# Turns at a shared port kept by semaphores, and a planner's times changed, in an attention and mixture-of-experts kernel

## The chip, the core and the metric

The kernel runs on one core of a Trainium2 chip. The core has five engines that run beside each other, each working through its own queue of instructions in order: TensorE (PE in the profile; PEld is its loading of weights), VectorE (DVE), ScalarE (ACT), GpSimd (POOL) and SyncE (SP, which here issues transfers). They wait for each other by semaphores. The metric is the device time of one execution in microseconds (us); lower is better.

## What is computed

Attention with a bias made of running sums, for 8 batches of 8 heads, 576 positions and 64 numbers a head, and then a layer of 8 experts. Each expert takes 576 of the 4608 tokens, in the order of the sorted gate logits:

```
scores = q @ k^T / 8;  cum = cumsum(max(s, 0))
scores = where(causal, -1e9, scores + min(cum_k - cum_q, 0))
attn   = exp(scores - rowmax);  x = (attn / (sum + 1e-9)) @ v          # 4608 x 512
logits = x @ w_gate                                                    # 4608 x 8
walk over all (token, expert) by falling logit: take it if the token is free and the expert has < 576
out[token] = relu(x[token] @ w1[expert]) @ w2[expert]
```

## The kernel before

Each fp32 number is split into a high and a low fp16 part, and products are summed from three half-precision products. ScalarE makes the high part, VectorE the low part, as a subtraction that reads two operands from SBUF; these are "the splits": line 411 for queries and keys (into QK), line 444 for values (Vl).

Attention goes over 16 head groups, each of two half passes (32 in all). A half pass n has these steps:

- `load` and `vload`: SP fetches raw, rv; ACT and DVE split them; SP moves halves of QK between partitions (line 416); QK gets rows of running sums by DMA (line 397, from auxk, which `sums` makes on DVE at the start, lines 346 to 360).
- `spass`: PE writes score tiles into three buffers pss (lines 486, 502), DVE takes each tile's row maximum (line 471, which also frees the buffer). ACT (lines 518, 520), POOL (line 522, tile mp), PE (524) and ACT (526) turn the maxima, and a DMA puts them into QK.
- `sts`: PE writes the transposed scores into pst (lines 544 to 547, 587 to 589), ACT takes the exponential (line 555, P), POOL subtracts its high part to get the low part R (line 557, two SBUF operands).
- `pv`: PE multiplies with the values (lines 618 to 620) into po; `norm`: ACT and DVE scale (lines 641 to 649), giving xp.
- `turn`: PE turns xp (line 681), ACT copies it (687), PE makes the logits (692, 693), DVE adds them (lines 700 and 707).

Of the router, parts for batches 0 to 3 and 4 to 6 (`choose`, lines 874 to 886) run on DVE inside attention. Behind attention come a router for the first expert (326 to 351 us) and eight experts, whose tokens POOL gathers (line 1226) and scatters (line 1352), with the router of the next expert on DVE beside PE's matmuls (lines 1293, 1297, 1379).

What sets every order: class `Plan`. The program adds tasks with an engine, a duration, what they need, a priority and buffers from rings; `run` then takes at each step the task that can start first by a clock of its own, and `start` emits its instructions. The order of each engine's queue is the order of `start`. A task with `lock` (each GpSimd task that is no DMA, the splits, most of `choose`, the sums, and the set-up work that may go to either engine) starts no earlier than the end of the other engine's last locked task, kept in `port`; this is in the plan alone, and nothing on the chip keeps that turn. Line 707 is not locked. One `Plan` makes attention, a second one router and experts.

## Time and profile before

| | us |
|---|---|
| median of 3 runs (lowest 775.1, highest 777.54) | 777.54 |
| the profiled execution | 777.66 |
| its span, first to last instruction | 775.6 |
| busy in it: PE, DVE, ACT, POOL | 722.0 (93%), 598.2 (77%), 391.7 (50%), 335.3 (43%) |

So 2.1 us lie around the span. Stages of the span: set-up and start-up to about 60 us, steady attention to about 312, its end to 326, the first expert's router to 351, the experts to 766, and the last scatter to the end. "Busy" is the time in which an engine has an instruction; the matmuls' ends are modelled and lie some 0.16 us behind their turns. An instruction that is held up at the port stays "busy", so a port stall is read from an instruction that lasts longer than its like, and a semaphore wait is read as idle time.

### The profile page before, as it was taken

The page shows a single profiled execution, that of the slowest core. Times are in us where ns is not written, and L with a number is a line of the kernel's source. Part 1 is how long each engine was busy: PE and PEld are TensorE (multiplying, and loading weights), DVE is VectorE, ACT ScalarE, POOL GpSimd, SP SyncE. Part 2 cuts the span into 40 slices and gives each one's busy share as a digit, 9 for nine tenths or more (in the row PEclk, how much of TensorE's full clock was granted, in tenths as well). Part 3 has the DMA queues.
Part 4 walks back from the last instruction along what each step waited for, and adds up shares of the span by engine and source line. Part 5 has one row for each costly group of instructions (what it writes and reads, how often), then busy time and mean ns, then how long its engine had stood idle before and what let it go on. Part 6 is the DMA issues. An engine that isn't in the chain of part 4 may idle for free.

```text
span 775.6 us, 22590 instructions
## 1 busy us (share of the span) xinstructions
PE 722.0 (93%) x8726; PEld 454.9 (59%) x8726; DVE 598.2 (77%) x2014; ACT 391.7 (50%) x794; POOL 335.3 (43%) x428
## 2 busy tenths in 40 slices
PE   9789999999999999628998999999999999999995
PEld 3457788787888888416644544545445454454542
DVE  7889999999999996678895877969788795380110
ACT  3548888888888878405334323324244232461110
POOL 7648988788878988102032041140412224202011
PEclk9679999999999999858999999999999999999998
DMA  7897768686776511106157376394845639851000
GB/s 233 195 213 202 220 175 250 172 241 196 209 203 171 156 35 64 63 35 204 42 167 200 110 113 180 129 222 133 190 156 155 187 105 262 228 180 48 15 28 34
DMA packets 89733, 118.72 MB, mean 153 GB/s; under 512 B 39246, under 2 KB 55758, under 8 KB 89614
## 3 DMA queue, kind: packets, MB, share of 16 engines
q1 hardware_dynamic: 83116, 97.82, 46.1%
q0 software_dynamic: 5952, 19.00, 8.1%
q8 instruction: 68, 1.11, 0.6%
q10 hardware_dynamic: 558, 0.47, 0.2%
q14 instruction: 39, 0.32, 0.1%
HBM read 71.67 MB, written 19.10 MB: 117 GB/s over the span
## 4 chain that ended last, share of the span: by engine, by line
PE 54%; issue 19%; DVE 13%; DMA 5%; POOL 4%; ACT 2%; SPq 1%; POOLq 0%; ACTq 0%; DVEq 0%
PE psm L1293 13%; PE psm L1379 10%; DVE pss L471 5%; PE pst L545 4%; PE pst L544 4%; PE pss L502 3%; PE po L618 3%; PE po L620 2%; PE po L619 2%; POOL out_dram L1352 2%; POOL xg L1226 2%; PE psn L1297 2%; PE po L735 2%; PE pss L681 2%; DMA xg<-xs,ids 1%
## 5 line engine op out<-in xcount | busy, mean ns | idle before, releaser
L557 POOL TENSOR_TENSOR R<-P 128x512 f16<-128x512 f32 (+1 forms) x221 | 218.9, 1016 | 26.9 <-ACT P L555 25.2
L1293 PE MATMUL psm<-xT,w1p 128*128 128x512 f16 (+1 forms) x876 | 193.1, 353 | 1.3 <-DMA xT<-xg 0.8
L1379 PE MATMUL psm<-w2p,hT 128*128 128x512 f16 x768 | 174.4, 379 | 0.0
L555 ACT ACTIVATE P<-pst 128x512 f32<-128x512 f32 (+1 forms) x224 | 119.9, 555 | 25.0 <-PE pst L547 10.3
L1297 PE MATMUL psn<-xT,w1p 128*128 128x64 f16 x768 | 129.7, 193 | 0.0
L471 DVE CUSTOM_DVE_ANT_0 pss<-pss,mS 128x512 f32<-128x512 f32 (+3 forms) x256 | 122.7, 506 | 9.0 <-PE pss L502 8.0
L1293 PEld LDWEIGHTS <-w1p 128*128 128x128 f16 x876 | 79.2, 98 | 80.0 <-issue 1.9
L1352 POOL DMA_INDIRECT out_dram<-y,ids x40 | 39.8, 995 | 198.7 <-ACT y L1390 169.6
L1379 PEld LDWEIGHTS <-hT 128*128 128x128 f16 x768 | 69.0, 98 | 80.3 <-issue 4.4
L1226 POOL DMA_INDIRECT xg<-xs,ids x40 | 43.6, 1089 | 167.3 <-DVE ids L1184 67.3
L618 PE MATMUL po<-V,P 128*128 128x65 f16 x960 | 113.8, 196 | 1.4 <-DVE xp L649 1.0
L620 PE MATMUL po<-V,R 128*128 128x65 f16 x960 | 114.0, 194 | 0.4 <-POOL R L557 0.4
L619 PE MATMUL po<-Vl,P 128*128 128x64 f16 x960 | 113.6, 193 | 0.0
L544 PE MATMUL pst<-QK 70*128 70x64 f16 (+4 forms) x512 | 108.5, 252 | 1.2 <-ACT P L555 0.7
L545 PE MATMUL pst<-QK 128*128 128x64 f16 (+4 forms) x512 | 107.8, 251 | 0.0
L619 PEld LDWEIGHTS <-P 128*128 128x128 bf16 x960 | 90.0, 100 | 9.1 <-issue 2.8
L618 PEld LDWEIGHTS <-P 128*128 128x128 bf16 x960 | 90.4, 98 | 5.9 <-issue 1.8
L1313 ACT ACTIVATE hT<-psm 128x512 f16<-128x512 f32 x64 | 38.2, 597 | 108.1 <-PE psm L1293 88.3
L620 PEld LDWEIGHTS <-R 128*128 128x128 f16 x960 | 89.9, 97 | 0.6 <-POOL R L557 0.6
L1390 ACT ACTIVATE y<-psm 128x512 f32<-128x512 f32 x32 | 19.1, 597 | 122.0 <-PE psm L1379 108.1
L502 PE MATMUL pss<-QK 67*128 67x512 f16 (+3 forms) x256 | 72.6, 307 | 4.7 <-DVE mr L471 2.4
L1297 PEld LDWEIGHTS <-w1p 128*128 128x128 f16 x768 | 67.7, 98 | 1.3
(221 smaller groups left out, 1443.4 us busy)
## 6 DMA issues: line engine op xcount, KB each, us to landing
QK<-QK SPq DMA_DIRECT2D x120, 144.0 KB
wst<-in_w_dram SPq DMA_DIRECT2D x32, 512.0 KB
wst<-in_w_dram SPq DMA_DIRECT2D x64, 256.0 KB
raw<-in_q_dram SPq DMA_DIRECT2D x32, 288.0 KB
raw<-in_k_dram SPq DMA_DIRECT2D x32, 288.0 KB
rv<-in_v_dram SPq DMA_DIRECT2D x32, 288.0 KB
xs<-xp SPq DMA_DIRECT2D x32, 256.0 KB
xs<-xp SPq DMA_DIRECT2D x8, 128.0 KB
```

The source lines that it names most:

```text
L471: return pl.add("v", dur, lambda: nc.vector.tensor_tensor_reduce(ps(), ps(), mask, 1.0, init() if init else -3e38, OP.add, OP.max, mr.t[:, ...
L502: nc.tensor.matmul(ps.t[:, :n], F()[:, q0:q0 + 128], F()[:, k0:k0 + n], start=True, stop=True)
L544: nc.tensor.matmul(ps[:, c0:c0 + n], F()[:, ks:ks + 128], F()[:, q:q + n], start=True, stop=False)
L545: nc.tensor.matmul(ps[:, c0:c0 + n], G()[:, ks:ks + 128], G()[:, q:q + n], start=False, stop=not diag)
L555: e = pl.add("a", n / 1200 + 0.171, lambda: nc.scalar.activation(P.t[:, c0:c0 + n], ps.t[:, :n], AF.Exp, scale=1.0 / YS), [x] + fresh, pri ...
L557: sub = lambda eng: eng.tensor_tensor(R.t[:, c0:c0 + n], P.t[:, c0:c0 + n], strided_hi(P.t)[:, c0:c0 + n], op=OP.subtract)
L618: nc.tensor.matmul(o[:, i], H[:, c:c + 128], V.t[:, pr, sl], start=f, stop=False)
L619: nc.tensor.matmul(o[:, i, 0:64], H[:, c:c + 128], Vl.t[:, pr, sl], start=False, stop=False)
L620: nc.tensor.matmul(o[:, i], R.t[:, c:c + 128], V.t[:, pr, sl], start=False, stop=l)
L1293: nc.tensor.matmul(ps[:, tiles[0]:tiles[-1] + 1] if len(tiles) > 1 else ps[:, tiles[0]], lhs(f, c, a), xT.t[:, tiles[0]:tiles[-1] + 1, 4 * ...
L1297: nc.tensor.matmul(pt.t[:, 64 * f:64 * f + 64], lhs(f, c, a), xT.t[:, 4, 4 * b + c, 0:64], start=s, stop=e)
L1379: nc.tensor.matmul(py.t, hT.t[:, f, a, 128 * i:128 * i + 128], w2p.t[:, f, b], start=f == 0 and k == 0, stop=f == 7 and k == 2)
```

## The change

Three things change, all in `Plan`. First, the clock of the plan: a PE task lasts 1.6% longer, a step from PE to ACT and from ACT to POOL 0.05 us longer and from DVE to PE 0.01 us longer (`AFTER`), and the port comes free for the other engine 0.06 us later (`HAND`). Second, since these numbers set the order, queues of all five engines are re-ordered, in attention and in the experts (there POOL's order stays). Third, in attention's plan alone, each locked task's last instruction gets a dependency on the other engine's last locked instruction, which becomes a semaphore wait where no other wait implies it.

```diff
+    HAND = 0.06
+    tc = None
+    AFTER = {("t", "a"): 0.05, ("a", "p"): 0.05, ("v", "t"): 0.01}
...
+        self.held = dict(v=None, p=None)
...
         if e == "t":
-            return dur, dur + 0.19
+            return dur * 1.016, dur * 1.016 + 0.19
...
+        made = f()
         if x.lock and e in "vp":
-            self.port[e] = t + x.occ
+            self.port[e] = t + x.occ + self.HAND
+            if self.tc:
+                other = self.held["p" if e == "v" else "v"]
+                if other is not None:
+                    self.tc.add_manual_dep(made.ins, other.ins.name, mybir.DependencyInfo(
+                        mybir.DependencyClass.Sync, mybir.DependencyReason.SCHED_ONLY), reason="port")
+                self.held[e] = made
         self.count -= 1
-        f()
...
-            y.ready = max(y.ready, t + x.occ if order else x.end)
+            y.ready = max(y.ready, t + x.occ if order else x.end + self.AFTER.get((e, y.e), 0.0))
...
         self.pl = Plan()
+        self.pl.tc = tc
```

Lines of the kernel before are 11 higher in the changed one from about line 225 on (411 is 422, 444 is 455, 471 is 482, 557 is 568), and 3 to 10 higher ahead of that.

Place 1, DVE's queue in the start-up, where the sums (lines 357, 358), the first splits and the first row maximum stand. Before:

```order
L357 SCALAR_TENSOR_TENSOR xp0_117<-xp0_117 64x576 [waits DVE_49]
L258 MEMSET P1_102 128x64
L358 TENSOR_SCALAR xp0_117<-xp0_117 64x576 [waits DVE_49]
L258 MEMSET V1_96 128x18
L411 SCALAR_TENSOR_TENSOR QK0_91<-raw0_87,QK0_91 128x576 [waits DMAHW1_49,Activation_49]
L411 SCALAR_TENSOR_TENSOR QK0_91<-raw0_87,QK0_91 128x576 [waits DMAHW2_49,Activation_49]
L411 SCALAR_TENSOR_TENSOR QK0_91<-raw0_87,QK0_91 128x576 [waits DMAHW3_49,Activation_49]
L411 SCALAR_TENSOR_TENSOR QK0_91<-raw0_87,QK0_91 128x576 [waits DMAHW4_49,Activation_49]
L285 TENSOR_SCALAR QK1_92<-mZ_131,vec_138 6x2560
L471 ISA pss0_122,mr0_105<-pss0_122,mS_130 128x128 [waits PE_49,Pool_49]
```

The same place after:

```order
L368 SCALAR_TENSOR_TENSOR xp0_117<-xp0_117 64x576 [waits DVE_49]
L296 TENSOR_SCALAR QK1_92<-mZ_131,vec_138 6x2560
L369 TENSOR_SCALAR xp0_117<-xp0_117 64x576 [waits DVE_49]
L422 SCALAR_TENSOR_TENSOR QK0_91<-raw0_87,QK0_91 128x576 [waits DMAHW3_49,Activation_49]
L422 SCALAR_TENSOR_TENSOR QK0_91<-raw0_87,QK0_91 128x576 [waits DMAHW4_49,Activation_49]
L309 MEMSET QK1_92 128x8x64 [waits DVE_49]
L455 SCALAR_TENSOR_TENSOR Vl0_98<-rv0_89,V0_95 128x1152 [waits DMAHW1_49,DMAHW4_49,Activation_49,Pool_49]
L422 SCALAR_TENSOR_TENSOR QK1_92<-raw1_88,QK1_92 128x2x576 [waits DMAHW6_49,DMAHW5_49,Activation_49]
L482 ISA pss1_123,mr0_105<-pss1_123,mS_130 128x128 [waits PE_49]
```

The first value split and the first split of QK1 moved ahead of the first row maximum (before they stood behind 16 of them), and the set-up rows of QK1 and two splits moved in between the sums.

Place 2, SP's queue in the start-up, around the first moves inside QK1. Before:

```order
L440 DMA rv1_90<-in_v_dram 128x576 [waits DMAHW3_49]
L327 DMA wgf_137<-in_w_gate_dram 128x4x8 [waits DMAHW4_49]
L440 DMA rv0_89<-in_v_dram 128x576 [waits DMAHW6_49,DVE_49]
L416 DMA QK1_92<-QK1_92 64x2x576 [waits DMAHW7_49,Activation_49]
L416 DMA QK1_92<-QK1_92 64x2x576 [waits DMAHW0_49]
L416 DMA QK1_92<-QK1_92 64x2x576 [waits DMAHW1_49,Activation_49]
```

After:

```order
L427 DMA QK0_91<-QK0_91 64x576 [waits DMAHW3_49]
L427 DMA QK0_91<-QK0_91 64x576 [waits DMAHW4_49]
L427 DMA QK1_92<-QK1_92 64x2x576 [waits DMAHW6_49,Activation_49]
L427 DMA QK1_92<-QK1_92 64x2x576 [waits DMAHW0_49]
L427 DMA QK1_92<-QK1_92 64x2x576 [waits DMAHW2_49,Activation_49]
```

The moves of QK1 stood behind a second load into rv0, which waits for DVE's value split; now they stand right behind those of QK0, and that load comes 13 rows later.

Place 3, DVE's queue in the middle of attention, around the seventh value split. Before:

```order
L471 ISA pss0_122,mr1_106<-pss0_122,mS_130 128x256 [waits PE_49]
L471 ISA mr1_106 128x1
L471 ISA pss2_124,mr1_106<-pss2_124,mS_130 128x512 [waits PE_49]
L471 ISA mr1_106 128x1
L444 SCALAR_TENSOR_TENSOR Vl0_98<-rv0_89,V0_95 128x1152 [waits DMAHW7_49,DMAHW0_49]
L649 TENSOR_TENSOR xp1_118<-po1_129,xp1_118 128x5x64 [waits Activation_49]
```

After:

```order
L660 TENSOR_TENSOR xp1_118<-po1_129,xp1_118 128x5x64 [waits Activation_49]
L482 ISA pss2_124,mr2_107<-pss2_124,mS_130 128x256 [waits PE_49]
L482 ISA mr2_107 128x1
L455 SCALAR_TENSOR_TENSOR Vl0_98<-rv0_89,V0_95 128x1152 [waits DMAHW3_49,DMAHW2_49,Pool_49]
L422 SCALAR_TENSOR_TENSOR QK0_91<-raw0_87,QK0_91 128x2x576 [waits DMAHW5_49,DMAHW2_49]
L422 SCALAR_TENSOR_TENSOR QK0_91<-raw0_87,QK0_91 128x2x576 [waits DMAHW7_49,DMAHW0_49]
L482 ISA pss0_122,mr2_107<-pss0_122,mS_130 128x512 [waits PE_49]
```

The splits stood one by one among the row maxima (2 pairs in 44 places behind the start-up); now 7 triples, 6 pairs and 11 single ones, the first of a row waiting for POOL. Behind the start-up 22 of DVE's instructions in attention have a new wait for POOL.

The other side, POOL's queue near the same place, after:

```order
L568 TENSOR_TENSOR R1_104<-P1_102 128x512 [waits PE_49,Activation_49]
L533 TENSOR_TENSOR mp1_111<-ms1_109,mp1_111 128x10 [waits Activation_49,Pool_49]
L568 TENSOR_TENSOR R1_104<-P1_102 128x512 [waits Activation_49] x2
L568 TENSOR_TENSOR R1_104<-P1_102 128x512 [waits DVE_49,Activation_49]
L568 TENSOR_TENSOR R1_104<-P1_102 128x512 [waits Activation_49] x2
```

One R task in such a row now waits for DVE's last split; 21 of POOL's instructions have such a wait, where before none in steady attention had one.

## Rows read from the trace of the kernel before

**Rows 1.** Windows: length, busy us (instructions) PE PEld DVE ACT POOL, granted clock, DMA share, GB/s.
```profile
36.00:47.20 11.20, 10.15 (x86) 6.94 (x87) 9.90 (x34) 3.76 (x7) 6.26 (x10) 0.50 0.89 211
...
60.00:312.00 252.00, 249.28 (x4893) 206.05 (x4891) 240.35 (x797) 213.66 (x500) 209.92 (x232) 1.00 0.62 175
...
420.00:766.00 346.00, 343.12 (x2476) 170.13 (x2474) 223.80 (x756) 111.24 (x182) 70.40 (x101) 1.00 0.51 141
```

**Rows 2.** Waits of PE, 60 to 312 us: us in total, times, longest.
```profile
PE po L618 <- DVE xp L649: 1.0, 2, 0.6
PE po L692 <- DVE xp L649: 0.6, 1, 0.6
PE pst L544 <- ACT P L555: 0.3, 1, 0.3
PE pss L502 <- ACT mt L526: 0.2, 1, 0.2
PE pss L502 <- DVE mr L471: 0.2, 1, 0.2
```

**Rows 3.** The chain that ended last, shares by line, 60:140 and then 226:312.
```profile
by line: DVE pss L471 25.0%; DVE QK L411 12.0%; DVE Vl L444 6.3%; DVE po L645 6.3%; issue 6.2%; DVE xp L649 5.2%; DVE mr L471 5.1%; PE pss L502 4.2%; PE pst L544 3.9%; PE po L618 3.7%; PE pst L545 3.4%; PE po L620 3.2%; PE po L619 3.1%; PE 
...
by line: PE pst L545 16.1%; PE pst L544 15.9%; PE po L618 11.5%; PE po L620 10.7%; PE po L619 10.5%; PE pss L502 10.3%; PE pss L681 6.5%; PE pst L547 5.3%; PE pss L486 4.5%; issue 1.5%; PE po L692 1.5%; ACT P L555 1.3%; PE po L693 1.3%; PE 
```

**Rows 4.** Single lines, 60:312: count, duration in ns min/median/max, first and last start.
```profile
L411 DVE SCALAR_TENSOR_TENSOR QK<-raw,QK x24: 1309/1351/2193, 73.3 to 277.3; 128x1152 f16<-128x1152 f32 x24
...
L444 DVE SCALAR_TENSOR_TENSOR Vl<-rv,V x14: 1314/1354/2150, 65.4 to 291.3; 128x1152 f16<-128x1152 f32 x14
...
L707 DVE TENSOR_TENSOR L<-L,L x7: 199/531/892, 97.3 to 301.5; 128x40 f32<-128x40 f32 x7
...
L875 DVE TENSOR_TENSOR eq<-L,m x2: 415/768/1120, 222.0 to 302.3; 128x160 f32<-128x160 f32 x1, 128x120 f32<-128x120 f32 x1
...
L879 DVE TENSOR_SCALAR sg<-m x2: 135/570/1004, 234.6 to 305.7; 128x20 int32<-128x20 int32 x1, 128x15 int32<-128x15 int32 x1
...
L557 POOL TENSOR_TENSOR R<-P x204: 392/1038/2153, 59.0 to 311.5; 128x512 f16<-128x512 f32 x88, 128x128 f16<-128x128 f32 x14
```

**Rows 5.** Groups by line and shape, 60:320 us: busy us, mean ns of one, idle before.
```profile
L411 DVE SCALAR_TENSOR_TENSOR QK<-raw,QK 128x1152 f16<-128x1152 f32 x24 | 33.9, 1415 | 0.0
...
L444 DVE SCALAR_TENSOR_TENSOR Vl<-rv,V 128x1152 f16<-128x1152 f32 x14 | 21.0, 1497 | 0.0
...
L707 DVE TENSOR_TENSOR L<-L,L 128x40 f32<-128x40 f32 x7 | 3.9, 551 | 0.2
```

**Rows 6.** Timelines at 81 to 84 us, DVE then PE: start, us, what, idle before it.
```profile
81.06 2.14 DVE L444 SCALAR_TENSOR_TENSOR Vl<-rv,V 128x1152 f16<-128x1152 f32 x1
...
83.66 0.17 PE L692 MATMUL po<-wgp,xt 128*128 128x16 f16 x1 [0.62 <-DVE xp L649]
```

**Rows 7.** The chain near the end of attention: a step from ACT (ends 314.04) to DVE.
```profile
314.04 0.02 issue
314.07 0.69 DVE R L557
```

**Rows 8.** Timeline of DVE in the start-up.
```profile
9.42 0.48 DVE L358 TENSOR_SCALAR xp<-xp 64x576 f16<-64x576 f32 x1
...
16.16 0.30 DVE L471 CUSTOM_DVE_ANT_0 pss<-pss,mS 128x128 f32<-128x128 f32 x1 [2.67 <-PE pss L502]
...
21.70 0.88 DVE L285 TENSOR_SCALAR QK<-mZ,vec 6x2560 f16<-6x2560 f16 x1
...
24.23 1.35 DVE L444 SCALAR_TENSOR_TENSOR Vl<-rv,V 128x1152 f16<-128x1152 f32 x1
```

**Rows 9.** The chain of the start-up.
```profile
26.72 6.87 DMA QK<-QK
...
33.60 2.46 DMA QK<-auxk
```

**Rows 10.** Waits of PE, 350 to 767 us.
```profile
PE psm L1241 <- DMA xg<-xs,ids: 4.6, 4, 1.7
```

## Prediction

> **What bounds the kernel now.** I read the windows first, because a share over the whole span hides the stages. In steady attention, 60 to 312 us, PE is busy 249.28 of 252.00 us at the full granted clock, and DVE 240.35 us; in the experts, from 420 us on, PE is busy 343.12 of 346.00 [rows 1]. PE is full in both, and DVE is close behind it in attention only. Nothing in this change removes PE work, so what it can give back there is PE's idle time, and I look for that next.
>
> In steady attention the shown idle time is 252.00 − 249.28 = 2.72 us, and 2.3 us of it are five kinds of waits, 7 times, mostly for DVE [rows 1, 2]. A matmul's modelled end lies some 0.16 us behind its turn, so each listed wait is read short by that: 2.72 + 7 × 0.16 = 3.8 us; gaps below 0.16 us don't show at all. The chain of waits says where these matter: from 60 to 140 us its largest lines are DVE's (25.0 + 12.0 + 6.3 + 6.3 + 5.2 + 5.1 = 60%), from 226 to 312 us its largest are all PE's, and POOL is among neither's [rows 3]. A DVE that is held up therefore costs time in the first third, and hardly any in the last.
>
> How DVE is held up is seen in its splits: the median key split takes 1351 ns and the longest 2193, a value split 1354 and 2150; R on POOL goes from 1038 to 2153 [rows 4]. The same instruction on the same shape does not take 0.8 us longer by itself: the other engine was in its way. One case from end to end: the value split at 81.06 takes 2.14 us, and PE, which waits for the xp step behind it, idles 0.62 us until 83.66 [rows 6]. So 0.8 us of stall became 0.6 us of PE idle (0.8 with the 0.16).
>
> **The change, part by part.** My sum is made against the profiled execution, 777.66 us, of which 775.6 are span; the median of the runs shown is 777.54, so the two agree and I add no correction.
>
> *Turns kept on the chip, steady attention.* What DVE loses there, mean less median or, where there are only two, longest less shortest: key splits 24 × (1.415 − 1.351) = 1.5 us; value splits 14 × (1.497 − 1.354) = 2.0; the router's eq 1.120 − 0.415 = 0.7 and sg 1.004 − 0.135 = 0.9 [rows 4, 5]. Together 5.1 us that come under turns. The logits' sum, line 707, loses 7 × (0.551 − 0.199) = 2.5 us more [rows 4, 5]; it isn't locked in either plan, so this stays. The Trainium skill (SBUF — State Buffer, section "SBUF: two separate sides") says that a DVE instruction with two SBUF operands competes with GpSimd for a pair of ports, which whoever starts first holds for its whole instruction. By that rule line 707 needs a turn as much as the splits do; the trace agrees, since its row runs from 199 to 892 ns [rows 4], and the sum would gain up to 1.2 us more with a turn there, which this change doesn't give.
>
> POOL's own stalls I price at zero, since POOL is not on the chain [rows 3]; what covers them is POOL's waiting time, and if that were gone R would come late for PE's line 620.
>
> Of 5.1 + 2.5 = 7.6 us of DVE stall PE felt at most 3.8. The turns cover two thirds of it: a gain of 2.5 us. Bounds: 5.1 us, if DVE carries the chain throughout; zero, if the stalls only turn into semaphore waits of the same length.
>
> *What the waits cost.* 22 DVE instructions get a wait for POOL, and behind each stand, on DVE's queue, the row maxima that free PE's three score buffers. If POOL is done by then, a wait costs about a hop; the nearest row is a step from ACT to DVE, 314.04 to 314.07 [rows 7]: 22 × 0.03 = 0.7 us of DVE time, a third to a half of it on PE's path like the stalls, 0.3 us. If POOL is late, DVE waits for the rest of an R, at most 1.04 us [rows 4], where before it would have gone first; that end is a rival below. The 21 waits on POOL stand ahead of R, whose user is PE's line 620; by the same argument as POOL's stalls, nothing.
>
> *Re-ordering, steady attention.* Splits now stand in twos and threes. This halves the number of turns, and it stops the row maxima for 3 × 1.35 = 4.05 us at a time instead of 1.35 [rows 4]. I price it at nothing, since PE has transposed scores and value products to do meanwhile; if these run out, it is a loss (rivals).
>
> *Re-ordering, start-up.* This is the largest unknown. Against: DVE's sums, which end now at 9.42 + 0.48 = 9.90 us, get two set-up rows (0.88 each [rows 8]) and two splits of half the size (0.7 each, half of 1.35 [rows 4]) in front of their end, 3.2 us, and a wait for POOL's set-up, which now starts behind DVE's memsets; I take 1 us for it without a row. The first row maximum comes at 16.16 [rows 8] behind the DMAs of these sums; I expect it 3 to 4 us later, near 20 us. For: a set-up row of 0.88, a value split of 1.35 and a key split of 1.35 no longer stand between the row maxima from 21.70 on [rows 4, 8], 3.6 us; and the moves of QK1, issued so late that a transfer of 6.87 us and the next of 2.46 us carried the chain from 26.72 to 36.06 [rows 9], go out ahead of the load that held them. From 36 to 47 us PE ran at 0.50 of its clock [rows 1]; what was sparse in front of that stays sparse, only somewhat later, so I leave this as it is. The two sides nearly cancel; I take −0.5 us. Bounds: +4 (nothing regained) and −5 (the 9.3 us of transfers leave the chain, less 4).
>
> *End of attention.* One more router step on DVE there is of the kind of sg, which lost 0.9 us [rows 4]; the chain is shared among engines there, so −0.3 us, between 0 and −0.9.
>
> *Experts.* No waits are added there; PE's and DVE's tasks change places, POOL's do not. PE's idle time is 346.00 − 343.12 = 2.9 us from 420 on [rows 1], and the largest kind of wait, 4.6 us for gathered tokens [rows 10], hangs on POOL's queue, which is unchanged. I take 0, bounds ±2.
>
> Sum: −2.5 + 0.3 − 0.5 − 0.3 + 0 = −3.0 us; 777.66 − 3.0 = 774.7 us.
>
> **Rivals.** *No gain* (0.18): the stalls become waits. For it: from 226 us on PE alone is the chain [rows 3], and DVE's time is worth something in a third of attention; against it, the case at 81 us [rows 6]. Time: 774.7 + 2.5 = 777.2.
>
> *Slower* (0.22): splits in a row starve PE of score buffers. The place is DVE's queue in attention, 13 doubles or triples. The case at 81 us is its price: 0.8 us more of DVE made PE idle 0.6 us [rows 6], and a triple takes 2.7 us longer than one split. Were PE to lose 0.6 us at each of the 13, that is +7.8, less the 2.5 gained: 777.66 + 5.3 = 783 us. It decides from about 0.2 us at each (13 × 0.2 = 2.6), where the gain is used up. Against it: DVE has 252.00 − 240.35 = 11.7 us without work in that stretch [rows 1]. A start-up of +4 us would end near the same place, at 779 to 780.
>
> *More gained* (0.08): the start-up's transfers leave the chain, −5 instead of −0.5: 770.
>
> *The change does not do what it says*: many turns are kept by other waits already, and only the order counts; this gives a time inside the forecast's range, and I give it no chance of its own.
>
> **How the numbers follow.** Forecast 0.52: 774.7, own range 772 to 777. About 0.3% of 777.5, 2.3 us, is what a measurement can tell from no change, so faster means below 775.2 and slower above 779.9. Below 775.2 lie 0.7 of the forecast (0.36) and the 0.08: 0.44. Slower is the slower case, 0.22. The rest is 0.34. Range for 8 in 10: down to 769.5, which leaves out less than half of the larger gain, and up to 782.5, which leaves out rather more than a half of the slower case.
>
> **What would show it.** The longest key and value splits fall from 2.2 to under 1.5 us, and R's longest to near 1.1; line 718 (707 before) still ranges to 0.9. DVE's waits list POOL's R, by under 2 us over attention; if it is over 5, the slower rival holds, and PE's waits for the maxima (line 482) grow with it. PE's idle time in steady attention falls from 2.7 to near 1 us. The first row maximum starts near 20 us, and no transfers of QK1 carry the chain for 9 us behind it. From the last attention matmul to the last scatter the length stays within 2 us. I am wrong if attention ends later than the 326 us of before, or if it ends earlier as expected and the experts give it back.

## The result, and the profile after

The change made the kernel slower: 781.48 us (median of 20 executions) against 775.5 us for the kernel before beside it. The ratio is 1.0067, with a 95% interval of 1.0053 to 1.0082, so about 5.2 us. I had forecast 774.7 us, 3.0 us less than before. The profiled execution of the changed kernel took 778.81 us (span 776.8), 2.7 us less than its median; that of before took 777.66, 2.2 us more than this later median. The two traces show less of the loss than the medians do.

The windows of the changed kernel (length, busy us and instructions of PE, PEld, DVE, ACT, POOL, granted clock, DMA share, GB/s), to stand beside [rows 1]:

```profile
36.00:47.20 11.20, 10.22 (x159) 7.64 (x157) 10.92 (x41) 7.14 (x17) 7.29 (x14) 0.95 1.00 229
60.00:312.00 252.00, 248.04 (x4816) 202.93 (x4815) 235.08 (x774) 210.15 (x489) 187.45 (x229) 1.00 0.62 175
420.00:766.00 346.00, 342.47 (x2477) 170.21 (x2476) 223.27 (x758) 111.29 (x182) 72.11 (x101) 1.00 0.50 141
```

In steady attention PE is 1.24 us less busy than in [rows 1], which looks like nothing. Look at the counts: 4816 matmuls in 252 us, where before had 4893, 1.6% fewer. That is some 4 us of work. PE's busy time hides most of it, because a matmul that starts up to 0.16 us late still finds the one ahead of it "busy" by its modelled end. The busy time of PEld, the loading of weights, falls with the count, by 1.5% (206.05 to 202.93 us).

A better measure is therefore a nearly fixed piece of work: the products of R on PE (line 631, 620 before), numbered from 0, from number 100 to number 800. The columns are start and end, length, busy us and count of that line on PE and PEld, granted clock, DMA share, GB/s. Before:

```profile
76.19:281.77 205.58, 82.70 (x702) 65.11 (x701) 1.00 0.67 191
```

After:

```profile
74.75:284.74 209.99, 82.44 (x701) 65.00 (x701) 1.00 0.68 192
```

The same products take 210.0 us instead of 205.6, at the full granted clock in both: steady attention lost 4.4 us. Below I call this the stretch. It repeats well: it is 205.6 us in e4, whose attention is that of before, and 210.0 in e3 and h3, whose attention has the order of the changed kernel.

The port stalls themselves are gone. Single lines of the changed kernel from 60 to 326 us, and over the whole span for 718 (count, ns min/median/max, first and last start), beside [rows 4]:

```profile
L422 DVE SCALAR_TENSOR_TENSOR QK<-raw,QK x26: 1344/1352/1359, 63.1 to 277.3; 128x1152 f16<-128x1152 f32 x26
...
L455 DVE SCALAR_TENSOR_TENSOR Vl<-rv,V x14: 1344/1351/1359, 65.6 to 291.2; 128x1152 f16<-128x1152 f32 x14
...
L568 POOL TENSOR_TENSOR R<-P x206: 397/1041/1081, 59.1 to 317.1; 128x512 f16<-128x512 f32 x89, 128x128 f16<-128x128 f32 x14
...
L718 DVE TENSOR_TENSOR L<-L,L x8: 199/707/1124, 93.9 to 325.3; 128x40 f32<-128x40 f32 x8
```

No split lasts over 1.36 us and no R over 1.08, where 2.2 and 2.15 were the longest; line 718, which has no turn, still reaches 1.12. What came in their place is in POOL's waits, 60 to 312 us (us in total, times, longest). Those for DVE's splits and router steps are new:

```profile
POOL R L568 <- DVE QK L422: 9.8, 3, 4.1
POOL mp L533 <- DVE den L655: 6.0, 2, 3.2
POOL R L568 <- DVE Vl L455: 5.2, 2, 3.6
...
POOL R L568 <- DVE dg L895: 3.3, 1, 3.3
...
POOL mp L533 <- DVE QK L422: 3.0, 1, 3.0
```

And the chain of waits, 60 to 140 us and then 226 to 312, has POOL's R in it, with 13.2% and 10.3%, where [rows 3] had none in either:

```profile
by line: DVE pss L482 15.7%; POOL R L568 13.2%; DVE QK L422 10.1%; issue 8.7%; PE pst L555 4.5%; PE pst L556 4.5%; PE pss L513 4.5%; PE po L629 3.9%; PE po L631 3.5%; PE po L630 3.4%; DVE Vl L455 3.3%; DVE mr L482 2.9%; PE pss L692 2.8%; DV
...
by line: DVE pss L482 10.6%; POOL R L568 10.3%; DMA QK<-QK 7.8%; DMA raw<-in_k_dram 6.5%; PE pst L556 5.5%; PE pst L555 5.5%; issue 4.3%; PE po L629 4.1%; PE pss L513 3.8%; PE po L631 3.7%; PE po L630 3.7%; ACT P L566 3.2%; SPq L393 3.1%; D
```

My first theory was therefore that POOL, held back by the waits, is late with R. The experiments did not bear it out as the main cause.

### The profile page after: what moved, and what is told of

The parts are those of the page before. It is cut to its first block, busy times and chain, and to the rows that moved or that the text cites. A ratio compares the mean times of both kernels' runs of the same rounds, so it can differ in the third digit from the quotient of the medians.

```text
span 776.8 us, 22605 instructions
## 1 busy us (share of the span) xinstructions
PE 723.2 (93%) x8726; PEld 452.5 (58%) x8726; DVE 592.9 (76%) x2017; ACT 390.4 (50%) x794; POOL 309.4 (40%) x425
## 4 chain that ended last, share of the span: by engine, by line
PE 45%; DVE 18%; issue 17%; POOL 7%; DMA 6%; ACT 2%; SPq 1%; another core or an unknown queue 0%; POOLq 0%; DVEq 0%; ACTq 0%
PE psm L1304 13%; PE psm L1390 12%; DVE pss L482 5%; POOL R L568 4%; DVE QK L422 2%; PE pst L556 2%; PE pst L555 2%; POOL out_dram L1363 2%; PE po L629 2%; PE pss L513 2%; DMA QK<-QK 2%; PE psn L1308 2%; PE po L631 2%; PE po L630 2%; PE pss L692 1%
## 5 line engine op out<-in xcount | busy, mean ns | idle before, releaser
L568 POOL TENSOR_TENSOR R<-P 128x512 f16<-128x512 f32 (+1 forms) x223 | 204.9, 950 | 52.6 <-ACT P L566 27.8
L1363 POOL DMA_INDIRECT out_dram<-y,ids x40 | 41.9, 1048 | 216.5 <-ACT y L1401 193.0
L1304 PEld LDWEIGHTS <-w1p 128*128 128x128 f16 x876 | 79.4, 98 | 79.9 <-issue 1.5
L555 PE MATMUL pst<-QK 70*128 70x64 f16 (+4 forms) x512 | 105.9, 248 | 0.3 <-ACT P L566 0.2
L556 PE MATMUL pst<-QK 128*128 128x64 f16 (+4 forms) x512 | 105.1, 248 | 0.0
L513 PE MATMUL pss<-QK 67*128 67x512 f16 (+3 forms) x256 | 73.6, 308 | 6.3 <-DVE mr L482 5.4
L1326 DVE SCALAR_TENSOR_TENSOR hT<-psm,hT 128x512 f16<-128x512 f32 x64 | 43.9, 686 | 39.9 <-ACT hT L1324 39.0
```

Source lines behind the costliest of these rows:

```text
L513: nc.tensor.matmul(ps.t[:, :n], F()[:, q0:q0 + 128], F()[:, k0:k0 + n], start=True, stop=True)
L555: nc.tensor.matmul(ps[:, c0:c0 + n], F()[:, ks:ks + 128], F()[:, q:q + n], start=True, stop=False)
L556: nc.tensor.matmul(ps[:, c0:c0 + n], G()[:, ks:ks + 128], G()[:, q:q + n], start=False, stop=not diag)
L568: sub = lambda eng: eng.tensor_tensor(R.t[:, c0:c0 + n], P.t[:, c0:c0 + n], strided_hi(P.t)[:, c0:c0 + n], op=OP.subtract)
L1304: nc.tensor.matmul(ps[:, tiles[0]:tiles[-1] + 1] if len(tiles) > 1 else ps[:, tiles[0]], lhs(f, c, a), xT.t[:, tiles[0]:tiles[-1] + 1, 4 * ...
```

## The experiments

All figures together: the median, the median of the kernel before on the same chip beside it, the ratio with its interval, and from the profiled execution the start of product 100 and the stretch from 100 to 800.

| kernel | order, waits | us | before | ratio (95%) | 100 at | stretch |
|---|---|---|---|---|---|---|
| before | old, none | | | | 76.2 | 205.6 |
| after | new, both | 781.48 | 775.5 | 1.0067 (1.0053–1.0082) | 74.7 | 210.0 |
| e1 | new, none | 790.86 | 776.49 | 1.0179 (1.0145–1.0212) | 77.3 | 220.6 |
| e2 | old, both | 790.05 | 776.49 | 1.0179 (1.016–1.0197) | 82.5 | 209.5 |
| e3 | new in attention only, both | 781.31 | 776.49 | 1.0065 (1.0043–1.0087) | 74.6 | 210.0 |
| e4 | new in experts only, none | 776.01 | 776.49 | 1.0000 (0.9979–1.0021) | 73.6 | 205.6 |
| f1 | new, DVE's only | 793.6 | 776.88 | 1.0216 (1.0193–1.0238) | 75.3 | 222.3 |
| f2 | new, POOL's only | 777.52 | 776.88 | 1.0019 (0.9998–1.0039) | 73.2 | 209.6 |
| f3 | planned pause 0, both | 792.88 | 776.88 | 1.0206 (1.017–1.0242) | 83.8 | 213.8 |
| f4 | pause only, both | 783.05 | 776.88 | 1.0074 (1.0046–1.0103) | 73.6 | 213.8 |
| g1 | new, DVE's only behind 40 us | 772.69 | 773.02 | 0.9998 (0.9981–1.0015) | 72.7 | 210.3 |
| g2 | new, DVE's only up to 40 us | 774.67 | 773.02 | 1.0029 (1.0008–1.0049) | 74.3 | 209.5 |
| g3 | old, both behind 40 us | 778.76 | 773.02 | 1.0098 (1.0065–1.0131) | 74.9 | 209.2 |
| g4 | recorded times only, none | 778.91 | 773.02 | 1.01 (1.0064–1.0135) | 71.8 | 212.4 |
| h1 | new, both, short R | 775.74 | 775.18 | 1.0001 (0.9986–1.0016) | 77.6 | 207.6 |
| h2 | old, none, short R | 770.59 | 775.18 | 0.9943 (0.9924–0.9962) | 74.4 | 201.6 |
| h3 | new, DVE's only behind 17 us | 775.18 | 775.18 | 1.0000 (0.9981–1.0019) | 73.5 | 210.0 |
| h4 | new to 60 us, then old numbers, no waits | 782.39 | 775.18 | 1.0092 (1.0064–1.0121) | 72.3 | 213.6 |
| i1 | new, both, short splits | 772.01 | 773.48 | 0.9982 (0.9961–1.0003) | 76.1 | 205.6 |
| i2 | old, none, short splits | 769.2 | 773.48 | 0.9931 (0.9906–0.9956) | 74.1 | 201.0 |

"Both" are the waits on DVE and those on POOL; in g1, g2 and h3 POOL's are kept everywhere. Product 100 of the old order without waits came at 76.2 us in one profiled execution and at 73.6 in another (e4, whose attention is the same), so single start-ups differ by 2.6 us. The clock was fully granted over the stretch but for f1, f4 and h4, where 3.4 us of it ran at 0.50; that can be an estimated 1.7 us of their length at most. The profiled execution of f3 was 6 us above its median.

### Order, waits, or the experts' plan

All diffs but those of the controls are against the changed kernel; the old order is had by setting the three new numbers back.

**e1**: the new order without waits.

```diff
-        self.pl.tc = tc
+        self.pl.tc = None
```

> The changed kernel's order on every engine, without the added waits: no turn is kept on the chip. Turns theory (POOL, which waits for DVE's splits and then has a row of R to catch up, is on the chain now: 10.3% of the chain from 226 to 312 us where it had none): the time goes back to 775 to 777, R leaves the chain, and attention ends near 322.5 us instead of 324.9. Order theory (splits in rows of two to five starve PE, with or without waits): it stays at 780 to 782. Experts theory (the new times in the experts' plan): it also stays at 780 to 782, but with attention's end near 322.5.

Measured: 790.86 us, 14.4 above before, outside all three expectations. All three took the waits as the cost or the order as a smaller one; in fact the waits repair 9 us of what the new order does without them. Its splits, by line and shape from 60 to 320 us (busy us, mean ns):

```profile
L422 DVE SCALAR_TENSOR_TENSOR QK<-raw,QK 128x1152 f16<-128x1152 f32 x26 | 41.8, 1634 | 0.0
L455 DVE SCALAR_TENSOR_TENSOR Vl<-rv,V 128x1152 f16<-128x1152 f32 x14 | 22.3, 1592 | 0.0
```

In [rows 5] the means are 1415 and 1497 ns. Against the median of 1.35 us the splits lose 26 × 0.28 + 14 × 0.24 = 10.6 us here and 3.5 us before. PE now waits for the row maxima behind them, 60 to 312 us (us, times, longest), of which [rows 2] had 0.2:

```profile
PE pss L513 <- DVE mr L482: 4.2, 8, 0.6
PE po L629 <- DVE xp L660: 2.2, 3, 1.3
```

So when nothing keeps POOL at rest, an order that is planned in turns, with rows of splits during which POOL is meant to rest, loses three times as much of its splits' time in meetings with R as the old one.

**e2**: the old order with waits.

```diff
-    HAND = 0.06
+    HAND = 0.0
...
-    AFTER = {("t", "a"): 0.05, ("a", "p"): 0.05, ("v", "t"): 0.01}
+    AFTER = {}
...
-            return dur * 1.016, dur * 1.016 + 0.19
+            return dur * 1.0, dur * 1.0 + 0.19
```

> The order of the kernel before on every engine, with waits that keep the turns in it (47 turns of DVE). Turns theory: slower than before by 3 to 6 us, 779 to 781, with POOL's waits for DVE's splits among the largest of POOL and R on the chain. Order theory and experts theory: 774 to 776, no slower than before, and the longest split under 1.5 us.

Measured: 790.05 us, 13.6 above before and far more than the turns theory had. The direction is right, the size is not. Two places carry most of it: product 100 comes at 82.5 us, and the stretch is 209.5. One turn of it, POOL and then DVE:

```profile
146.20 3.04 POOL L568 TENSOR_TENSOR R<-P 128x512 f16<-128x512 f32 x3
150.77 1.40 POOL L568 TENSOR_TENSOR R<-P 128x512 f16<-128x512 f32 x2 [1.53 <-ACT QK L420]
...
149.27 1.36 DVE L422 SCALAR_TENSOR_TENSOR QK<-raw,QK 128x1152 f16<-128x1152 f32 x1 [0.48 <-POOL R L568]
```

R ends at 149.24, the split starts at 149.27 and ends at 150.63, and R goes on at 150.77 (the row names ACT as what POOL waited for; the split's end is the nearer event): 0.03 us towards DVE, 0.14 towards POOL, and 1.53 us of POOL idle for one split. R is the largest line of its chain from 76 to 300 us:

```profile
by line: POOL R L568 30.5%; DVE pss L482 8.6%; DVE QK L422 7.3%; PE pst L556 5.3%; PE pst L555 5.2%; issue 4.7%; PE pss L513 4.5%; PE po L629 3.6%; PE po L631 3.3%; PE po L630 3.3%; DVE Vl L455 3.2%; DVE po L656 2.4%; PE pss L692 2.3%; DVE 
```

**e3 and e4**: the new numbers in one of the two plans, with the factor 1.016 made an attribute `SLOW`. In e3 they are off in the experts' plan:

```diff
-    pl = Plan()
+    pl = Plan(); pl.HAND, pl.AFTER, pl.SLOW = 0.0, {}, 1.0
```

In e4 they are off in attention's, which has no waits either:

```diff
-        self.pl = Plan()
-        self.pl.tc = tc
+        self.pl = Plan(); self.pl.HAND, self.pl.AFTER, self.pl.SLOW = 0.0, {}, 1.0
+        self.pl.tc = None
```

> Attention as in the changed kernel, waits and all; the experts are planned with the numbers of before. Turns theory and order theory: 779 to 782, as the changed kernel. Experts theory: 775 to 777.

> Attention as in the kernel before, without waits; only the experts are planned with the new numbers. Turns theory and order theory: within 1.5 us of the kernel before, 774 to 777. Experts theory: 779 to 782, the whole loss.

Measured: 781.31 and 776.01 us. The loss is in attention's plan; the experts' new order is worth nothing that can be told from zero (±1.6 us).

### Which waits, and which number

**f1 and f2**: one of the two kinds of waits; f1 is shown, f2 has `"p"` in place of `"v"`.

```diff
-                if other is not None:
+                if other is not None and e == "v":
```

> The changed kernel's order on every engine; of the two kinds of added waits only those on DVE are left (a split waits until POOL's planned R are done; R waits for no split). The order without any wait took 790.9, with both kinds 781.5. If the 9 us lie with POOL, which without a wait starts R in the middle of a row of splits (R stretched by 28.5 us and the splits by 10.8 in attention), this stays at 788 to 791. If they lie with DVE starting its splits too early, this is near 782.

> The same with only POOL's waits left (R waits for the planned splits, a split waits for nothing). If POOL starting too early is what the 9 us are, 780 to 783, splits above 1.35 us only where one starts behind an R that runs. If POOL's idle time behind the waits (3 to 4 us at each row of splits) is what makes the changed kernel 4.4 us longer than before from the 100th to the 800th product of R, this is no better than 781 and the chain still has R on POOL.

Measured: 793.6 and 777.52 us, the first 2.6 us above its range, the second 2.5 below. POOL's waits take 12 us off the new order (1.0179 to 1.0019), as expected of POOL starting too early. DVE's waits cost 4 us beside POOL's (1.0019 to 1.0067); without POOL's it is 3 us (1.0179 to 1.0216), which lies within the intervals. In f2 POOL's R is not among the largest lines of the chain any more, 76 to 300 us:

```profile
by line: DVE pss L482 10.7%; PE pst L555 9.1%; PE pst L556 8.9%; PE pss L513 7.5%; PE po L629 7.4%; PE po L631 6.7%; PE po L630 6.5%; DVE QK L422 5.3%; PE pss L692 4.8%; issue 4.1%; PE pss L497 3.5%; PE pst L558 3.0%; DVE mr L482 2.3%; DVE 
```

Yet its stretch is 209.6, nearly as long as with R on the chain. The second half of f2's expectation, R still on the chain, failed; this was the first sign against my theory of POOL.

**f3 and f4**: the pause alone taken out (`HAND = 0.0`), and the pause alone kept (`AFTER = {}`, 1.016 to 1.0).

> The changed kernel with the planned pause between turns at 0 instead of 0.06 us: waits, recorded times and all else kept. The turns go back from rows of two to five splits to mostly single ones. Theory of the number of turns (each turn leaves POOL idle some 1.5 us for a split and the way there and back, 0.03 us towards DVE and 0.14 us towards POOL, which the plan doesn't have at 0): as with the order of before with waits, 787 to 791. Theory of long rows (rows of splits are what costs): 774 to 778.

> The other half: the planned pause of 0.06 us and the waits are kept, the recorded times (the factor 1.016 on PE's steps and the additions to PE-ACT, ACT-POOL and DVE-PE) are left out. Theory of the number of turns: 779 to 783, near the changed kernel, since the rows of splits come from the pause. If the recorded times are what made the order with waits better than the order of before with waits (790.1 to 781.5): 786 to 791.

Measured: 792.88 and 783.05 us, which bears out the theory of the number of turns, though both lie above their ranges. With waits, the pause of 0.06 us is what makes the new order bearable. It gathers splits into fewer turns: by the traces, the 40 splits behind 60 us take 40 turns in f3, 14 in f4 and 17 in the changed kernel. But the stretch is 213.8 us in f3 and in f4, so the number of turns did not set it; f3 lost its time in the start-up (product 100 at 83.8 against 73.6) and behind product 800. What the recorded times add to the pause can't be told from nothing by the medians (1.0074 without them, 1.0067 with); the stretch is 3.8 us longer without them, up to 1.7 of that by the clock.

### Where the waits cost

**g1, g2 and h3**: DVE's waits only at some of the plan's times t. g1 is shown; g2 has `t <= 40.0`, h3 `t > 17.0`.

```diff
-                if other is not None:
+                if other is not None and (e == "p" or t > 40.0):
```

> The changed kernel without the waits that DVE's steps planned in the first 40 us have for POOL (set-up and first splits); all other waits and the order are kept. All DVE waits together cost 4 us (777.5 without them, 781.5 with). If these 4 us lie in the start-up, where a set-up row of DVE waits 3.9 us for POOL's set-up, 777 to 779. If they lie with the splits in attention, each held until POOL is through its R, 780 to 782.

> The complement: DVE's waits for POOL are kept in the first 40 us only, POOL's waits everywhere. If DVE's waits cost in the start-up, 780 to 782; if they cost in attention, 777 to 779.

> The changed kernel without the waits of DVE's steps planned in the first 17 us, which all wait for one and the same step of POOL's set-up; only the first of them, a set-up row of QK, shows as a wait, of 3.9 us. If this one wait makes up the start-up's share: as without all waits of the first 40 us, within 1.5 us of before. If the later ones of the start-up are needed too: 3 to 5 us slower than before.

Measured, as ratios to before: 0.9998, 1.0029 and 1.0000, where the changed kernel has 1.0067. (The absolute expectations of g1 to g4 were set at another chip's level; before took 773.02 beside them.) Without DVE's early waits the loss is gone, and to leave out those of the first 17 us is enough for it (h3). But g2, which keeps the early waits and leaves out the late ones, loses only 2.2 us, as its expectation had it for the other case. So g1 and h3 put the loss in the start-up, g2 puts it in attention: either half of DVE's waits costs next to nothing beside POOL's (f2 has 1.0019), and only both together cost 4 to 5 us. Why they add up so is not shown.

Of the waits of the first 17 us only one shows as a wait of any length, in DVE's timeline of the changed kernel:

```profile
7.01 0.88 DVE L296 TENSOR_SCALAR QK<-mZ,vec 6x2560 f16<-6x2560 f16 x1 [3.93 <-POOL W L822]
```

and the same row in h3:

```profile
4.06 0.88 DVE L296 TENSOR_SCALAR QK<-mZ,vec 6x2560 f16<-6x2560 f16 x1 [0.98 <-POOL vec L287]
```

A row of constants for QK, and with it the running sums and the first splits, stands behind the last step of POOL's early set-up, a table W that only the router uses. The first row maximum (line 482 on DVE, 0 to 60 us), which started at 16.16 us before [rows 8], starts at 22.1 us in the changed kernel:

```profile
L482 DVE CUSTOM_DVE_ANT_0 pss<-pss,mS x46: 276/504/732, 22.1 to 58.2; 128x128 f32<-128x128 f32 x12, 128x384 f32<-128x384 f32 x12, 128x256 f32<-128x256 f32 x11, 128x512 f32<-128x512 f32 x11
```

and at 20.0 in h3:

```profile
L482 DVE CUSTOM_DVE_ANT_0 pss<-pss,mS x48: 275/506/734, 20.0 to 59.3; 128x128 f32<-128x128 f32 x12, 128x256 f32<-128x256 f32 x12, 128x384 f32<-128x384 f32 x12, 128x512 f32<-128x512 f32 x12
```

**g3**: the old order with waits behind 40 us only.

> The order of the kernel before with both kinds of waits, but only on steps planned behind the first 40 us. With waits from the start it took 790.1, of which by its trace some 6 to 8 us were lost before the 100th product of R, 4 us up to the 800th and 2 us behind. If the turns of the start-up are what costs there, 781 to 784, with the 100th product back at 74 to 76 us. If the early loss comes from later waits (single turns of 1.5 us of POOL each), 787 to 790.

Measured: 778.76 beside 773.02, 5.7 by the medians and 7.6 by the ratio. Product 100 is back at 74.9, so the start-up's turns cost the old order 7.6 us by these two traces, and 6.3 by the ratios of e2 and g3. The stretch stays at 209.2: waits alone, in the old order, make it 3.6 us longer than before, and the new order with waits is only 0.8 us longer still.

**g4**: no waits, no pause, recorded times only (`HAND = 0.0`, `self.pl.tc = None`).

> No waits, and no planned pause between turns; only the recorded times (1.016 and the additions) shape the order. Theory of long rows: the order without waits costs 14 us because the pause draws the splits into rows in which POOL was planned to rest and doesn't; without the pause the splits stand mostly single and meet R as seldom as before, so 774 to 778. If it is the recorded times, or any new order, that brings the meetings, 785 to 791.

Measured: 778.91 beside 773.02, between the two expectations. Without waits, the pause adds 6 us to the loss (1.01 to 1.0179), but an order shaped by the recorded times alone already loses 7.7, with a stretch of 212.4.

### What the steady part lost

**h1 and h2**: R on 384 of its 512 columns, with turns and, as the control, in the kernel before.

```diff
-            sub = lambda eng: eng.tensor_tensor(R.t[:, c0:c0 + n], P.t[:, c0:c0 + n], strided_hi(P.t)[:, c0:c0 + n],
-                                                op=OP.subtract)
+            s = slice(c0, c0 + 3 * n // 4 if n == 512 and n0 > 1 else c0 + n)
+            sub = lambda eng: eng.tensor_tensor(R.t[:, s], P.t[:, s], strided_hi(P.t)[:, s], op=OP.subtract)
```

> The changed kernel, order and waits kept, but from the third pair of heads on each R of 512 columns is made on 384 of them, so part of R keeps an older pair's values (the output is wrong by that). POOL's R falls from 1.04 to some 0.8 us and POOL has time in hand behind each turn. Theory of POOL's lost time (POOL idles 3 to 4 us at each row of splits and its backlog is what makes the stretch from the 100th to the 800th product of R 210.0 us where it was 205.6): the stretch falls to 204 to 206, the time by 4 to 6 us against the changed kernel, and R leaves the chain. Theory of the order (PE's and DVE's new order costs it, POOL or not): the stretch stays at 208.5 to 210, the time within 2 us of the changed kernel's (5 us above before).

> The control: the same short R in the kernel before, no waits (the output is wrong in the same part). POOL is not on its chain, so the theory of POOL's lost time expects little, a gain of 0 to 2 us from fewer meetings with the splits; a gain as large as the one with turns would say that POOL's load bounds both.

Measured: 0.66% off with turns (1.0067 to 1.0001), and 0.57% off in the control. The stretches, with turns and then in the control:

```profile
77.58:285.17 207.59, 82.44 (x701) 65.00 (x701) 1.00 0.68 194
```

```profile
74.37:276.00 201.63, 82.51 (x702) 65.11 (x701) 1.00 0.68 195
```

With turns the time fell by 5.1 us, as the theory of POOL's lost time had it, but the stretch only by 2.4, half as far as that theory wanted. And the control gains as much, and the gap between the stretches grew from 4.4 to 6.0 us. So POOL's lost time is not shown to be what sets the two kernels apart. What the control gained is seen in its splits, 60 to 320 us:

```profile
L422 DVE SCALAR_TENSOR_TENSOR QK<-raw,QK 128x1152 f16<-128x1152 f32 x24 | 32.5, 1357 | 0.0
...
L455 DVE SCALAR_TENSOR_TENSOR Vl<-rv,V 128x1152 f16<-128x1152 f32 x14 | 18.9, 1348 | 0.0
```

In [rows 5] the means are 1415 and 1497 ns. With the shorter R the splits lose almost nothing any more, without a single wait, and the stretch is 3.9 us shorter. That is close to the 3.8 us of idle time that the prediction had found in PE.

**i1 and i2**: the splits on half of their elements, with turns and in the kernel before.

```diff
-            lo = [pl.add("v", 0.15 + n * S / 960, lambda t=t, a=a, z=z: stt(
-                part(A_, 1, t, 1 - t, a, z), raw.t[:, t, a:z], QS, part(A_, 1, t, t, a, z), op0=OP.mult,
+            lo = [pl.add("v", 0.15 + n * S / 960, lambda t=t, a=a, z=z, w=S if g < 4 else S // 2: stt(
+                part(A_, 1, t, 1 - t, a, z)[..., :w], raw.t[:, t, a:z, :w], QS, part(A_, 1, t, t, a, z)[..., :w], op0=OP.mult,
...
-        lo = pl.add("v", 0.15 + 2 * S / 960, lambda: nc.vector.scalar_tensor_tensor(
-            Vl.t, rv.t, VS, V.t[:, :, :, 0:64], op0=OP.mult, op1=OP.subtract), [hi], prio=t0 - 2, uses=[rv, V, Vl], lock=True)
+        lo = pl.add("v", 0.15 + 2 * S / 960, lambda w=2 if g < 3 else 1: nc.vector.scalar_tensor_tensor(
+            Vl.t[:, :w], rv.t[:, :w], VS, V.t[:, :w, :, 0:64], op0=OP.mult, op1=OP.subtract), [hi], prio=t0 - 2, uses=[rv, V, Vl], lock=True)
```

> The changed kernel, order and waits kept, but from the fifth group of key splits and the fourth of value splits on each is made on half of its elements (the output is wrong by that): a split falls from 1.35 to some 0.75 us and a row of three from 4.0 to 2.3. Theory of rows of splits (they hold up the row maxima and the xp steps behind them on DVE, and PE waits for those): the stretch from the 100th to the 800th product of R falls from 210.0 to 203 to 205 us, 3 us more than in the control, and the time comes to within 2 us of the control's. If PE's new order itself, with whatever it waits for, costs the 4 us: the gap to the control stays 4 to 6 us.

> The control: the same half splits in the kernel before, without waits (the output is wrong in the same part). The splits stand mostly single here and meet R less often when short: the stretch falls from 205.6 to 202 to 204 us, the time by 2 to 4 us.

Measured: 0.85% and 0.69% off. The stretches:

```profile
76.06:281.65 205.59, 82.45 (x700) 65.01 (x701) 1.00 0.70 197
```

```profile
74.08:275.12 201.04, 82.50 (x703) 65.14 (x701) 1.00 0.69 195
```

The gap stays at 4.6 us, so the length of the rows of splits is not the cause either. Where the 4.4 us of the changed kernel lie can be read from its trace. First, the stretch is not quite the same work. Over all of PE (length, busy us and instructions of PE, PEld, DVE, ACT, POOL), before and then after:

```profile
76.19:281.77 205.58, 203.14 (x3945) 167.00 (x3942) 201.92 (x679) 175.49 (x409) 171.13 (x189) 1.00 0.67 191
```

```profile
74.75:284.74 209.99, 206.37 (x3956) 168.00 (x3954) 203.13 (x674) 176.56 (x410) 153.51 (x188) 1.00 0.68 192
```

By their starts it is 3939 and 3951 matmuls: the new order does a few more transposed scores between products 100 and 800, an estimated 0.9 us by the pace of their like. Second, PE starts late more often. Call a start late that comes more than 0.06 us behind the pace of its like (the faster quarter of the same step ahead of the same line, in the traces of before and after). Then before has 22 late starts with 4.8 us, after 43 with 8.5 us. The 0.9 and the 3.7 us make up the 4.4, less 0.2 for smaller differences.

By the last semaphore event ahead of each, 3.5 us of the late starts after stand behind things that made hardly any start late before (0.06 us): DVE's sum of the logits (line 711), for whose buffer po the value products wait, 1.3 us; POOL's mp 0.9; ACT's P 0.7; and ACT's value split or DVE's scaling of po, which are too close to tell apart, 0.7. Behind the row maxima stand 2.7, where before had 2.3. The logits' sum and P stay as they are or grow in h1 (1.3 and 1.4 us) and in i1 (1.2 each), so neither could close the gap. The old order with waits (g3) has 45 late starts with 8.9 us, 5.3 of them behind the row maxima. So with waits both orders start late by as much, at different places, and the new order alone can't be named as the cause. No run changes one of these places by itself.

### A version better than both

**h4**: planned as after up to 60 us, behind that with the old numbers and no waits.

```diff
+        new = t < 60.0
...
-            self.port[e] = t + x.occ + self.HAND
+            self.port[e] = t + x.occ + self.HAND * new
...
-                if other is not None:
+                if other is not None and new and (e == "p" or t > 17.0):
```

The factor 1.016 and `AFTER` are switched in the same way.

> Up to 60 us planned as in the changed kernel, with its waits but for those of the first 17 us on DVE; behind that planned with the numbers of before and without waits. If the new start-up is worth its 2 us (100th product of R at 72.7 us without DVE's early waits, 73.6 to 76.2 before) and the rest can be had as before (205.6 us to the 800th): 1 to 3 us faster than before. If any other order without waits meets more often than before's: 2 to 8 us slower.

Measured: 782.39 beside 775.18. The start-up is good (product 100 at 72.3), but the plan that goes on from there isn't the old order, and its stretch is 213.6. Its splits, 60 to 320 us, lose about as much to R as those of [rows 5], but R itself loses more. The splits and R of h4, and then R of before (1038 ns is its median [rows 4]):

```profile
L425 DVE SCALAR_TENSOR_TENSOR QK<-raw,QK 128x1152 f16<-128x1152 f32 x26 | 37.5, 1447 | 0.0
...
L458 DVE SCALAR_TENSOR_TENSOR Vl<-rv,V 128x1152 f16<-128x1152 f32 x14 | 21.1, 1507 | 0.0
```

```profile
L571 POOL TENSOR_TENSOR R<-P 128x512 f16<-128x512 f32 x171 | 197.8, 1178 | 27.7 <-ACT P L569 26.4 <-ACT den L655 0.6 <-PE po L634 0.2
```

```profile
L557 POOL TENSOR_TENSOR R<-P 128x512 f16<-128x512 f32 x176 | 190.7, 1106 | 21.3 <-ACT P L555 19.7 <-PE po L693 1.2
```

So another order of the same planner with the same numbers is 8.0 us longer in the stretch, up to 1.7 of that by the clock. Its R loses 171 × 0.14 = 24 us to meetings, where before lost 176 × 0.07 = 12, so the second expectation fits, and an order that costs so much without more meetings is not shown. No kernel that computes the whole was shown to be faster than before; g1 and h3 equal it.

## Why the prediction was wrong

**The turns' gain** (−2.5). This is the step that failed. The stalls themselves went as said: the longest split is 1.36 us, the longest R 1.08. The Trainium skill (SBUF — State Buffer, section "SBUF: two separate sides") says that the port is held for a whole instruction by whoever starts first; the lines agree, 2.2 us without turns and 1.36 with, and line 718, which has none, up to 1.12. The stalls were also worth about what I took: with them gone and no waits (h2), the stretch is 3.9 us shorter, though R is shorter there too. What failed is the step from stalls ended by waits to time gained. In the old order, where nothing else changes, waits made the stretch 3.6 us longer (g3), beyond my bound of zero. At worst, I had thought, the stalls would become waits of the same length; but POOL's waits came on top, and PE's late starts behind the row maxima grew from 2.3 to 5.3 us. (The router's eq and sg I had compared across two shapes each; against the same shapes with turns they had lost 1.7 us, where I took 1.6, which changes nothing.)

**What the waits cost** (+0.3). The hop is right, 0.03 us towards DVE. Two things were missed. POOL's waits, which I priced at nothing behind POOL's idle time, put 1.53 us of idle time on POOL for a single split, and brought R onto the chain. By h1 and f2 this is not the main thing that PE felt, but POOL's mp, which stands in the same queue, made PE late by 0.9 us. And DVE's waits cost 4 us beside POOL's (f2 to after).

**Re-ordering, steady attention** (priced at nothing). It fails or holds with the waits. Without them the new order costs 14 us (e1), recorded times alone 7.7 (g4). With them, the stretch is 210.0 against 209.2 in the old order with waits, and 0.9 us of this is more work. I had priced a row of splits by what it holds up on DVE, and excused it by PE's other work; I had not seen that the order decides how often R and the splits meet, and which of PE's steps start late.

**Re-ordering, start-up** (−0.5; of it +1 for a wait "without a row"). That wait took 3.9 us, and the first row maximum started at 22.1, not near 20; in h3, where the same row waits 1.0 us, at 20.0. A transfer of QK still carries the chain, so [rows 9] did not leave it:

```profile
20.04 6.31 DMA QK<-QK
```

I had left the clock "as it is", and it did not stay so. The time at a granted clock of 0.50 (1.2 of 2.4 GHz) is 20.5 us before and 13.7 after, and lies earlier (columns as in [rows 1]):

```profile
26.80:47.30 20.50, 17.63 (x142) 11.81 (x141) 16.84 (x48) 10.42 (x19) 12.76 (x16) 0.50 0.89 190
```

```profile
23.40:37.10 13.70, 11.11 (x46) 4.51 (x46) 12.23 (x44) 3.86 (x9) 5.11 (x18) 0.50 0.78 201
```

From 36 to 47 us PE did 159 matmuls at 0.95, where before had 86 at 0.50. By product 100 the changed kernel is level with before (74.7 against 73.6 to 76.2).

**End of attention and experts** (−0.3 and 0). From product 800 to the last logits matmul it is 40.2 us after and 40.8 before, a gain of 0.6; e4 puts the experts at 1.0000 (±0.0021). Both terms hold. Attention ends later all the same: its last logits matmul ends at 324.9 us, against 322.6 before, and a later end was my sign of being wrong.

**The rivals.** The slower rival had the sign and, with 783 us, nearly the figure; the figure is luck, since its mechanism, PE starved of score buffers by rows of splits, is seen only without waits (4.2 us of waits for line 482 in e1). With waits, in the new order, PE's listed waits for that line are 0.2 us, 60 to 312 us:

```profile
PE po L629 <- DVE xp L660: 1.1, 3, 0.5
PE po L629 <- DVE L L711: 0.5, 2, 0.4
PE po L703 <- ACT V L453: 0.5, 1, 0.5
...
PE pss L513 <- DVE mr L482: 0.2, 1, 0.2
```

and i1 left the gap as it was. The rival "no gain", stalls turned into waits, had the mechanism nearer, but not the loss. My sign for the slower rival, over 5 us of DVE's waits for R, didn't show either; they are 2.3 us from 60 to 312 us.

**How PE was read.** I added 0.16 us to each listed wait to find 3.8 us of idle time, and expected the shown idle time to fall from 2.7 to near 1 us; it rose to 4.0 (252.00 − 248.04). The count of matmuls in the window was the better row: it fell by 1.6% while busy time fell by 0.5%.

**What stays open.** The steady part's late starts are placed, but no run took one of the places away, so what each is worth by itself is not shown. Nor is it shown why DVE's early and late waits cost 4 to 5 us only together. And the sum of the medians: the traces show some 3.8 us (0 in the start-up, 4.4, −0.6) of the 5.2, and for h3 some 1 to 4 us (0 to 3 gained in the start-up, 4.4 lost, 0.6 gained) where the medians show none. The granted clock goes some way to explain this: in the changed kernel the five executions with the lowest mean clock (0.954 to 0.959) took 781.6 to 784.1 us, the six with the highest (0.965 to 0.967, the profiled one among them) 776.8 to 781.3, and the mean over all executions is 0.962 there and 0.965 in h3. Which of the two, clock or time, follows the other is open.

## What to carry over

A planner's order and the waits that keep it are one thing: either without the other cost this kernel 8 to 14 us. That stalls are worth 4 us does not mean that waits which end them gain anything: here the waits cost PE more late starts than the stalls had. Before putting real waits on a planned exclusion, look at what the first waits of the program stand behind; to leave out those of the first 17 us, one of them a constant row behind a table that nobody needed yet, took the changed kernel back to the time of before. And measure a stage of a PE-bound kernel by the time of a fixed number of matmuls, not by PE's busy time, and count what else stands between them.

## What was not expected of the hardware

The way there and back is not the same: a wait on DVE for POOL ended 0.03 us behind POOL's instruction, a wait on POOL for DVE 0.14 us behind DVE's. In e2's trace this holds for each of the 25 splits in front of which DVE idled, and for 35 of POOL's 47 waits behind a split. And POOL's time counts where POOL is on no chain: cutting R by a quarter gave the kernel before, whose chain had no R [rows 3], 4.4 us. The splits of that run lose almost nothing to R any more, so fewer meetings at the port are the likely way; R itself was shorter too, and no run parts the two.
